# Attention and two feed-forward layers on one core: key and query loads that write all 128 partitions, and a planner that counts 16 transfer engines and instruction fetches

## The chip, the cores and the metric

The kernel runs on one core of a Trainium2 chip, as one program. The metric is the device time of that program in microseconds (us). TensorE (PE in the profile; its weight loads are PEld) does the matrix products; VectorE (DVE), ScalarE (ACT) and GpSimd (POOL) do the rest; SyncE (SP) computes nothing and issues nearly all transfers (DMAs).

## The reference

Attention with two small mixes over the heads, then two feed-forward layers:

```python
scores = scale * np.matmul(q, k.transpose(0, 1, 3, 2))      # 4 x 12 x 448 x 448, head_dim 64
scores = np.einsum('bhij,hg->bgij', scores, w_pre)          # mix over heads
attn = np.exp(scores - scores.max(-1, keepdims=True))
attn = attn / (attn.sum(-1, keepdims=True) + 1e-09)
attn = np.einsum('bhij,hg->bgij', attn, w_post)             # mix over heads
x = np.matmul(attn, v)                                      # to 1792 x 768
h = x @ moe_w_in; g = where(h>=1, h, where(h<=-1, 0, (h+1)**2/4)); x = g @ moe_w_out
h = x @ moe2_w_in; solu = h * softmax(h); x = layernorm(solu) * g_ln @ moe2_w_out
```

## The kernel before

**Two stages.** The attention takes about the first 375 us, the two feed-forward layers the rest. The feed-forward code is not touched by the change, and the text below is on the attention.

**Chunks and tiles.** Four batches of 448 query rows are cut into four chunks each (110, 110, 110 and 118 rows), 16 chunks in all. For a chunk:

- `qk` makes the scores of its 12 heads on PE, two heads at a time: one head's 64 rows of the key and query tiles lie in partitions 0 to 63, the other's in 64 to 127. In the kernel before the two are heads p and p+6. ACT (in chunk 0 also DVE) copies each head's scores out of PSUM (`qk_evac`).
- `remap` moves the copied scores, by one DMA for each head (192 in all), into a tile `sr` in which the 12 heads of one query row lie in neighbouring partitions. It reads 110 or 120 rows and writes 10 partitions.
- `pre` mixes the heads of two query groups (five rows each side) at once on PE. DVE takes the row maximum (`rmax`), ACT the exponential (`expo`), POOL and DVE the normalisation (`guard`, `norm`, `wscale`).
- `post` mixes again on PE: 28 small products in a row, 112 instructions. `evac` copies them out, `av` multiplies with the values, and `store_x` writes the result.

**Words.** All these products are in 32-bit float. One of them is four PE instructions in the program: two weight loads and two products, so the trace has two product records for one product. In the planner's table `WORDS`, a `qk` of two heads or a `pre` is 16 instructions, a `post` 112. PE's instructions come to the core in blocks of 256 (16 KB), by transfers that the profile shows as a queue of kind "instruction". The built program also holds PE instructions that only wait for a semaphore (254 before the change, 272 after it); the planner's table leaves them out.

**The loads.** `load_k` brings the keys of four heads in two DMAs of 64 partitions each; three such loads make a batch. `load_q` brings a chunk's queries, also as two DMAs of 64 partitions. Both are issued on SP, those for chunk 0's queries on ACT. Between the products, `spin` puts 430 ns dummy products on PE in the first two chunks.

**What sets the order.** Every operation is a `Task` with an engine, an estimated duration, a due time (priority) and dependencies; `Order.emit` runs a list scheduler over them and writes each engine's instructions in the order that comes out. The due times and gates are computed from the table `OFFS`, the tile counts stand in `BUFS`. In the kernel before the planner models the transfers as two wires (`wire`, `XFER`), and a block of instructions as landing a fixed time (`FETCH`, 4800 ns) after the one before it.

## Time and profile before

| | before |
|---|---|
| median of 3 runs | 1055.34 us (1051.85 to 1056.74) |
| the profiled execution | 1054.95 us |
| its span from the first to the last instruction | 1053.2 us |
| PE busy | 1021.6 us, 97% of the span |
| DVE, ACT, POOL busy | 750.0, 623.2, 352.6 us |
| mean granted TensorE clock | 0.990 |

The profiled execution is 0.39 us below the median of the runs, and 1.75 us of it lie outside the span. Busy time is the time in which at least one instruction of the engine was running; the idle time of an engine before an instruction is put down to what released that instruction, and "issue" means that nothing that the profile shows was waited for.

### The profile page before, as it was taken

How to read it: one execution, taken by the hardware profiler on the slowest of the kernel's cores; microseconds unless marked ns; L12 is line 12 of the kernel's file. 1: busy time of each engine (PE TensorE's matmuls, PEld its weight loads, DVE VectorE, ACT ScalarE, POOL GpSimd, SP SyncE). 2: the span in 40 equal slices, each digit the busy share in tenths (PEclk: the TensorE clock that was granted, in tenths of full speed). 3: DMA queues.
4: the chain of work that ended last, by engine and by line, in shares of the span. 5: the costliest groups of instructions: out<-in, count | busy, mean ns of one | idle time of the engine just before them, and what ended most of it. 6: DMA issues, size and time to landing. Idle time of an engine off the chain costs nothing.

```text
span 1053.2 us, 27458 instructions
## 1 busy us (share of the span) xinstructions
PE 1021.6 (97%) x11103; PEld 844.0 (80%) x11103; DVE 750.0 (71%) x1258; ACT 623.2 (59%) x1329; POOL 352.6 (33%) x470
## 2 busy tenths in 40 slices
PE   8989998998999999999999999999999999999998
PEld 4555655565665799999999999999999888889998
DVE  3545564655656882588987869898887999888863
ACT  3868885886977675543334434343434577688761
POOL 4111121212211352454555445554521255033210
PEclk9989998999999999999999999999999999999999
DMA  7786676687757450332424232433364646598321
GB/s 187 215 190 191 194 209 194 179 235 200 231 179 231 152 187 21 98 122 81 140 70 140 91 120 90 143 111 102 115 207 163 211 174 242 186 334 315 118 81 60
DMA packets 91358, 171.42 MB, mean 163 GB/s; under 512 B 10220, under 2 KB 66016, under 8 KB 91232
## 3 DMA queue, kind: packets, MB, share of 16 engines
q1 hardware_dynamic: 90816, 169.30, 51.5%
q8 instruction: 88, 1.44, 0.6%
q10 hardware_dynamic: 160, 0.34, 0.2%
q14 instruction: 38, 0.31, 0.1%
q0 software_dynamic: 256, 0.02, 0.0%
HBM read 91.07 MB, written 39.85 MB: 124 GB/s over the span
## 4 chain that ended last, share of the span: by engine, by line
PE 91%; issue 2%; DVE 2%; ACT 2%; DMA 2%; POOL 1%; ACTq 0%; SPq 0%; DVEq 0%; POOLq 0%
PE ps_post L406 7%; PE ps_o L878 7%; PE ps_o L879 7%; PE ps_o L877 7%; PE ps_h L848 7%; PE ps_h L847 7%; PE ps_h L849 7%; PE ps_pre L370 7%; PE ps_av L457 6%; PE ps_qk L336 6%; PE ps_ot L1211 3%; PE ps_ot L1212 3%; PE ps_ot L1213 3%; PE ps_h L1211 3%; PE ps_h L1213 3%; PE ps_h L1212 3%
## 5 line engine op out<-in xcount | busy, mean ns | idle before, releaser
L406 PEld LDWEIGHTS ps_post<-wr,p 64*64 64x64 f32 x5040 | 105.0, 138 | 50.3 <-issue 35.7
L375 DVE TENSOR_REDUCE nm<-ps_pre 128x1 f32<-128x448 f32 x180 | 105.5, 618 | 48.3 <-PE ps_pre L370 45.8
L878 PE MATMUL ps_o<-g,wout 128*128 128x448 f32 x384 | 139.3, 363 | 0.0
L877 PE MATMUL ps_o<-g,wout 128*128 128x448 f32 x384 | 139.1, 362 | 0.0
L879 PE MATMUL ps_o<-g,wout 128*128 128x448 f32 x384 | 138.8, 362 | 0.0
L380 ACT ACTIVATE p<-ps_pre,nm 128x448 f32<-128x448 f32 x180 | 113.1, 637 | 27.1 <-DVE nm L375 26.9
L406 PE MATMUL ps_post<-wr,p 64*64 64x60 f32 x5040 | 106.7, 223 | 13.1 <-issue 12.0
L869 POOL TENSOR_TENSOR g<-t,g 128x448 fp32r<-128x448 f32 x64 | 83.2, 1303 | 100.9 <-ACT g L865 84.1
L887 DVE TENSOR_TENSOR x2acc<-ps_o,x2acc 128x448 f32<-128x448 f32 x168 | 100.2, 616 | 20.9 <-PE ps_o L879 19.6
L766 POOL TENSOR_TENSOR m<-m,v 128x768 f32<-128x768 f32 (+1 forms) x48 | 86.7, 1806 | 80.8 <-DVE v L748 54.3
L370 PE MATMUL ps_pre<-sr,wp 64*64 64x448 f32 (+1 forms) x720 | 100.9, 569 | 5.5 <-ACT at L426 3.2
L336 PE MATMUL ps_qk<-kraw,qb 64*64 64x448 f32 (+2 forms) x768 | 97.2, 543 | 5.7 <-issue 3.8
L354 ACT ACTIVATE s<-ps_qk 119x448 f32<-119x448 f32 (+1 forms) x186 | 91.0, 562 | 17.4 <-PE ps_qk L336 15.6
L387 POOL TENSOR_SCALAR nm<-nm 128x2 f32<-128x2 f32 x90 | 18.5, 206 | 235.3 <-ACT p L380 234.8
L853 ACT ACTIVATE t<-ps_h,st 128x448 f32<-128x448 f32 x64 | 40.4, 631 | 81.4 <-PE ps_h L849 76.7
L738 ACT ACTIVATE v<-v,st 128x768 int32<-128x768 int32 (+1 forms) x48 | 42.2, 880 | 58.0 <-DVE v L734 57.7
L877 PEld LDWEIGHTS ps_o<-g,wout 128*128 128x128 f32 x384 | 72.0, 188 | 5.3 <-DVE x2acc L887 0.2
L878 PEld LDWEIGHTS ps_o<-g,wout 128*128 128x128 f32 x384 | 72.1, 188 | 4.6
L879 PEld LDWEIGHTS ps_o<-g,wout 128*128 128x128 f32 x384 | 72.0, 187 | 4.6
L428 DVE COPY at<-ps_post 128x420 f32<-128x420 f32 x94 | 55.8, 597 | 25.1 <-PE ps_post L406 20.7
L426 ACT ACTIVATE at<-ps_post 128x420 f32<-128x420 f32 x94 | 54.6, 587 | 31.9 <-PE ps_post L406 30.3
L457 PE MATMUL ps_av<-at,vv 128*64 128x240 f32 (+1 forms) x648 | 70.4, 358 | 0.0
(196 smaller groups left out, 2456.9 us busy)
## 6 DMA issues: line engine op xcount, KB each, us to landing
sr<-s SPq DMA_DIRECT2D x144, 192.5 KB
raw<-in_moe_w_out_dram SPq DMA_DIRECT2D x22, 768.0 KB
raw<-in_moe_w_in_dram SPq DMA_DIRECT2D x14, 768.0 KB
sr<-s SPq DMA_DIRECT2D x48, 210.0 KB
xe<-e SPq DMA_DIRECT2D x14, 512.0 KB
el<-xe SPq DMA_DIRECT2D x14, 512.0 KB
raw<-in_moe_w_in_dram SPq DMA_DIRECT2D x12, 512.0 KB
kraw<-in_k_dram SPq DMA_DIRECT2D x24, 224.0 KB
```

The lines of the kernel that those rows point to most:

```text
L336: nc.tensor.matmul(out=qk_t[b, c, p + 6 * e][64 * j:at_], lhsT=qb[rows, i % 2, lo:hi], rhs=kraw_t[b, p][rows], start=True, stop=True,)
L354: nc.scalar.activation(out=s[:n], in_=qk_t.pop((b, c, h))[:n], func=AF.Copy, scale=0.125)
L370: nc.tensor.matmul(out=pre_t[t][o:o + 64], lhsT=wp[k_], rhs=sr[i % 2][k_, g, :], start=True, stop=True)
L375: nc.vector.tensor_reduce(nm_t[t // 2][:, 0, t % 2:t % 2 + 1], pre_t[t], axis=AX.X, op=ALU.max, negate=True)
L380: nc.scalar.activation(out=p, in_=pre_t.pop(t), func=AF.Exp, bias=nm[:, 0, e], accum_out=nm[:, 1, e])
L406: nc.tensor.matmul(out=ps[i][64 * j:64 * j + 64, k, :], lhsT=ps_p[e][64 * i:64 * i + 64, x:x + 64], rhs=wr[64 * i:64 * i + 64, e], start=T ...
L457: nc.tensor.matmul(out=ps[0][64 * j:64 * j + 64, a, :2 * w].rearrange("p (e s c) -> p e s c", e=2, c=SEG), lhsT=v_t[b][:, 1 + m, h * D:(h ...
L766: nc.gpsimd.tensor_tensor(out=m, in0=m, in1=vt.pop(key).bitcast(F32)[:, :n], op=ALU.mult)
L877: nc.tensor.matmul(out=ps, lhsT=wh, rhs=g[:, 0], start=(i == 0), stop=False)
L878: nc.tensor.matmul(out=ps, lhsT=wh, rhs=g[:, 1], start=False, stop=False)
L879: nc.tensor.matmul(out=ps, lhsT=wl, rhs=g[:, 0], start=False, stop=(i == 1))
L887: nc.vector.tensor_tensor(out=dst, in0=op.pop((u, m)), in1=dst, op=ALU.add)
```

## The change

**Keys.** One DMA loads the keys of four heads into all 128 partitions. A unit of `qk` is now heads 2p and 2p+1, since these lie one above the other in the input. **Queries.** The rows of two neighbouring chunks lie side by side in the partitions: `load_q(i, w)` brings one third (four heads) of chunk i into partitions 0 to 63 and the same third of chunk i+1 into 64 to 127. So each chunk's queries are loaded twice, and one half of each copy is used: the even heads from the load of chunk i, the odd heads from that of chunk i-1. Three loads of 128 partitions stand for two of 64. **Spins.** Only one of the two heads of a unit brings a dummy product (10 instead of 20, beside the first five). **The plan.** A class `Wires` keeps 16 transfer engines with their busy times; each transfer costs so much on so many of them, a block of instructions is asked for 320 instructions ahead and goes on one engine of the table `BLOCK_ON`, behind what is queued there. The offsets are other numbers, key tiles go from five to four and `wr` from six to five.

```diff
-OFFS = dict(split=-19.802, pre=0.556, rmax=-10.082, expo=-14.671, guard=36.186, ...
+OFFS = dict(split=-19.802, pre=2.072, rmax=-10.221, expo=-12.343, guard=40.787, ...
-BUFS = dict(kraw=5, q=2, vv=2, s=12, sr=2, p=8, st=8, wr=6, x=3, psa=4, psb=4)
+BUFS = dict(kraw=4, q=6, vv=2, s=12, sr=2, p=8, st=8, wr=5, x=3, psa=4, psb=4)
-BLOCK, FETCH, AHEAD, SWITCH = 256, 4800, 32, 120
-LAND = 1300
-XFER = dict(load_k=lambda *a: (1500, 1200), load_q=lambda *a: (1200, 900), load_v=lambda *a: (1900, 1000),
-            remap=lambda i, b, c, h: (92 * GR[c], 0), e_load=lambda n: (3000, 2300), e_stash=lambda n: (1200, 1000),
+BLOCK, ASKED, PRELUDE, SWITCH = 256, 320, 62, 120
+LAND, DEEP = 1300, 8
+BLOCK_ON = {6: 4, 7: 5, 0: 6, 1: 7, 2: 12, 3: 13, 4: 14, 5: 15}
+XFER = dict(load_k=lambda *a: (1160, 16), load_q=lambda i, w: (650, 16), load_v=lambda b, m: (1000 if m else 1800, 16),
+            remap=lambda i, b, c, h: (72 * GR[c], 10), e_load=lambda n: (2200, 16), e_stash=lambda n: (1000, 16),
...
-                k, late = (sent + AHEAD) // BLOCK + 1, 0
-                while k * BLOCK <= sent + AHEAD + t.words:
...
+                t.dur += wire.fetch(st, t.work, t.words)
+            if e == 'SP':
+                t.dur += wire.room(st)
...
+class Wires:
+    def __init__(self):
+        self.busy, self.words, self.asked, self.out = [0] * 16, PRELUDE, {}, []
+
+    def send(self, at, load, starts):
+        cost, n = load
+        for e in range(n):
+            self.busy[e] = max(self.busy[e], at) + cost
+        end = max(self.busy[:n])
+        self.out += [end + LAND] * starts
+        return end
+
+    def room(self, at):
+        return max(0, self.out[-DEEP] - at) if len(self.out) >= DEEP else 0
+
+    def fetch(self, at, work, words):
+        a, late = self.words, 0
+        self.words += words
+        for x in range((a // 64 + 1) * 64, a + words + 1, 64):
+            t, k = at + late + work * (x - a) // words, (x + ASKED) // BLOCK
+            if (x + ASKED) % BLOCK == 0:
+                e = BLOCK_ON[k % 8]
+                self.busy[e] = max(t + 1200, self.busy[e], self.asked.get(k - 1, 0) - 1500) + 900
+                self.asked[k] = self.busy[e] + 1500
+            elif x % BLOCK == 0:
+                late += max(0, self.asked.get(x // BLOCK, 0) - t)
+        return late
...
     def load_k(b, p):
         t = pl['kraw'].tile([128, 2, S], F32, tag="kraw", name="kraw")
-        heads = k[b].rearrange("p (e d) s -> d (p e) s", e=2)
-        for e in range(2):
-            nc.sync.dma_start(out=t[e * D:(e + 1) * D], in_=heads[:, 6 * e + p:6 * e + p + 2])
+        nc.sync.dma_start(out=t, in_=k[b, p:p + 2].rearrange("j p s -> p j s"))
...
-    def load_q(i, b, c):
-        n = H // 2 * GR[c] * R
-        for e in range(2):
-            (nc.sync if i else nc.scalar).dma_start(out=qb[e * D:(e + 1) * D, i % 2, QPAD:QPAD + n], in_=q[b, c, :, e * n:(e + 1) * n])
+    def load_q(i, w):
+        r0, r1 = (64 if i < 0 else 0), (64 if i == last_q else 128)
+        wide = max(GR[i % 4] if i >= 0 else 0, GR[(i + 1) % 4] if i < last_q else 0) > 11
+        o = 44 * R * w
+        n = QW[w] if wide else 44 * R
...
+        (nc.sync if i > 0 else nc.scalar).dma_start(
+            out=qb[(i + 1) % 2 * 3 + w][r0:r1, at_:at_ + n], in_=q_rows[D * i + r0:D * i + r1, o:o + n])
...
-        for h in (p, p + 6):
+        for h in (2 * p, 2 * p + 1):
...
-                if i < 2 and p >= P['sp0']:
+                if i < 2 and p >= P['sp0'] and not e:
                     add("PE", 430, 1e6, spin, 1, b, c, h, deps=[a2], new=[r_psb], use=[(r_s, -1)])
```

Three places show what the new plan writes. The first is PE's order up to the first `pre`, before the change (a row is line, operation, tiles and shape; `x5` is five of them in a row):

```order
L336 MATMUL ps_qk<-kraw,qb 64x448
L336 MATMUL ps_qk<-kraw,qb 55x448
L345 MATMUL ps_spin<-s 64x256 x2
L336 MATMUL ps_qk<-kraw,qb 64x448
L336 MATMUL ps_qk<-kraw,qb 55x448
...
L345 MATMUL ps_spin<-s 64x256 x5
L370 MATMUL ps_pre<-sr,wp 64x448 x8
```

and after it:

```order
L370 MATMUL ps_qk<-kraw,qb_121 64x448
L370 MATMUL ps_qk<-kraw,qb_121 55x448
L370 MATMUL ps_qk<-kraw,qb_124 64x448
L370 MATMUL ps_qk<-kraw,qb_124 55x448
L379 MATMUL ps_spin<-s 64x256 x2
L404 MATMUL ps_pre<-sr,wp 64x448 x8
```

Before, 48 products of `qk` (both first chunks) and 24 spins (the first five among them) stand ahead of the first `pre`; now it is 40 and 13.

The second place is PE around its 1792nd instruction, where block 7 begins (in the last row of each excerpt); before:

```order
L406 MATMUL ps_post<-wr,p 64x60 x28
L336 MATMUL ps_qk<-kraw,qb 64x448
L336 MATMUL ps_qk<-kraw,qb 60x448
...
L370 MATMUL ps_pre<-sr,wp 64x448 x4
L406 MATMUL ps_post<-wr,p 64x60 x28
L336 MATMUL ps_qk<-kraw,qb 64x448
L336 MATMUL ps_qk<-kraw,qb 60x448
...
L406 MATMUL ps_post<-wr,p 64x60 x28
```

and after:

```order
L440 MATMUL ps_post<-wr,p 64x60 x28
L370 MATMUL ps_qk<-kraw,qb_121 64x448
L370 MATMUL ps_qk<-kraw,qb_121 60x448
...
L404 MATMUL ps_pre<-sr,wp 64x448 x8
L370 MATMUL ps_qk<-kraw,qb_121 64x448
L370 MATMUL ps_qk<-kraw,qb_121 60x448
...
L440 MATMUL ps_post<-wr,p 64x60 x84
```

Before, `post` always came alone (90 times 28 products). Now nine stand as pairs and two as threes, the one shown here among them.

The third place is SP's order where the second batch's keys are loaded, before:

```order
L315 DMA qb<-in_q_dram 64x660 x2
L359 DMA sr<-s 10x12x448 x6
L309 DMA kraw<-in_k_dram 64x2x448 x2
L359 DMA sr<-s 10x12x448 x4
L309 DMA kraw<-in_k_dram 64x2x448 x2
L359 DMA sr<-s 10x12x448 x2
L309 DMA kraw<-in_k_dram 64x2x448 x2
L315 DMA qb<-in_q_dram 64x660 x2
```

and after:

```order
L334 DMA kraw<-in_k_dram 128x2x448
L393 DMA sr<-s 10x11x448
L348 DMA qb_123<-in_q_dram 128x440
L356 DMA vv<-in_v_dram 128x768
L393 DMA sr<-s 10x11x448
L334 DMA kraw<-in_k_dram 128x2x448 x2
L348 DMA qb_124<-in_q_dram 128x440
L393 DMA sr<-s 10x12x448 x12
```

The key loads moved ahead of the last chunk's twelve remaps, and thirds of the queries stand between them.

## Rows read from the trace of the kernel before

**Rows 1.** The page: busy time by engine, instruction queue, chain by engine.
```profile
PE 1021.6 (97%) x11103; PEld 844.0 (80%) x11103; DVE 750.0 (71%) x1258; ACT 623.2 (59%) x1329; POOL 352.6 (33%) x470
...
q8 instruction: 88, 1.44, 0.6%
...
PE 91%; issue 2%; DVE 2%; ACT 2%; DMA 2%; POOL 1%; ACTq 0%; SPq 0%; DVEq 0%; POOLq 0%
```

**Rows 2.** Windows: stretch, length, busy time (instructions) by engine, clock, DMA share, GB/s.
```profile
0.00:375.00 375.00, 348.27 (x7658) 220.06 (x7658) 214.58 (x470) 278.72 (x755) 84.68 (x213) 0.97 0.71 198
375.00:1053.20 678.20, 673.28 (x3451) 623.95 (x3449) 535.42 (x788) 344.51 (x574) 267.96 (x258) 1.00 0.42 143
```

**Rows 3.** Waits of PE: line, released by: us in total, times, longest.
```profile
PE ps_post L406 <- issue: 12.0, 8, 4.5
PE ps_qk L336 <- issue: 3.8, 2, 3.2
```

**Rows 4.** Timeline of PE: start, length, instruction, records [idle before, released by].
```profile
51.69 0.93 PE L406 MATMUL ps_post<-wr,p 64*64 64x60 f32 x30
53.09 0.62 PE L406 MATMUL ps_post<-wr,p 64*64 64x60 f32 x26 [0.46 <-issue]
...
61.75 1.43 PE L406 MATMUL ps_post<-wr,p 64*64 64x60 f32 x42 [3.42 <-issue]
...
162.16 1.43 PE L406 MATMUL ps_post<-wr,p 64*64 64x60 f32 x41 [4.47 <-issue]
...
249.59 0.58 PE L336 MATMUL ps_qk<-kraw,qb 64*55 64x448 f32 x1 [3.18 <-issue]
```

**Rows 5.** DMA queues and issues from 51.6 to 59 us: no row of kind instruction.
```profile
q1 hardware_dynamic: 776, 1.48, 82.4%
...
sr<-s SPq DMA_DIRECT2D x4, 210.0 KB
...
qb<-in_q_dram SPq DMA_DIRECT2D x2, 165.0 KB
```

**Rows 6.** DMA queues from 58.9 to 60.3 us.
```profile
q8 instruction: 1, 0.02, 4.9%
```

**Rows 7.** Windows behind the three longest waits of rows 4.
```profile
61.80:71.50 9.70, 9.44 (x192) 6.28 (x194) 4.79 (x11) 4.33 (x11) 1.16 (x4) 0.54 0.77 184
...
162.20:167.00 4.80, 4.80 (x61) 3.13 (x65) 0.74 (x2) 1.76 (x5) 0.19 (x1) 0.56 0.57 175
...
249.70:258.00 8.30, 7.69 (x126) 4.48 (x126) 3.71 (x10) 4.52 (x15) 0.58 (x2) 1.00 0.83 227
```

**Rows 8.** Windows: 64-partition loads at the start, 128-partition loads from 375 us.
```profile
2.00:6.00 4.00, 4.00 (x11) 1.73 (x11) 0.00 (x0) 1.24 (x1) 4.00 (x8) 1.00 0.99 213
...
375.00:390.00 15.00, 15.00 (x108) 13.96 (x107) 11.61 (x16) 9.56 (x17) 7.91 (x8) 1.00 0.76 242
```

**Rows 9.** Timeline of SP at the start.
```profile
0.73 4.08 SPq L309 DMA_DIRECT2D kraw<-in_k_dram  x6
...
10.65 1.24 SPq L315 DMA_DIRECT2D qb<-in_q_dram  x2
12.00 7.71 SPq L359 DMA_DIRECT2D sr<-s  x9
```

**Rows 10.** Timeline of PE at the first `pre`.
```profile
23.98 2.10 PE L345 MATMUL ps_spin<-s 64*64 64x256 f32 x9
25.78 0.60 PE L370 MATMUL ps_pre<-sr,wp 60*64 60x448 f32 x3
```

**Rows 11.** The chain that ended last: start, us, engine, records; one transfer in it.
```profile
38.66 1.04 PE ps_post L406 x56
...
50.89 0.98 PE ps_pre L370 x8
...
86.46 1.50 PE ps_qk L336 x16
...
231.62 3.84 DMA sr<-s
```

More of the change, by code (lines that the diff above doesn't have):

```diff
@@ L105, in dma @@
         d.issue = t
-        d.load = XFER.get(fn.__name__, lambda *a: (xfer, xfer))(*a)
+        d.load = XFER.get(fn.__name__, lambda *a: (xfer, 16))(*a)
         return d
@@ L146, in emit @@
         avail, free = {}, {}
-        sent, landed, was, wire, slow = 0, {}, False, [0, 0], 0
+        was, wire, slow = False, Wires(), 0
         for t in self.tasks:
@@ L205, in give @@
                 if o.eng == 'DMA':
-                    wire[:] = [max(w, o.ready) + x if x else w for w, x in zip(wire, o.load)]
                     o.start = o.ready
-                    o.dur = max(w for w, x in zip(wire, o.load) if x) - o.ready
+                    o.dur = wire.send(o.ready, o.load, STARTS.get(t.fn[0].__name__, 1) if t.eng == 'SP' else 0) - o.ready
                     done.append(o)
@@ L264, in attention @@
     wk = const.tile([128, H, HR], F32, name="wk")
-    qb = const.tile([128, 2, QPAD + H // 2 * 120], F32, name="qb")
+    qb = [pl['q'].tile([128, QPAD + QW[w]], F32, name=f"qb{j}{w}") for j in range(2) for w in range(3)]
     at = const.tile([128, KB, H, 3 * SEG], F32, name="at")
@@ L271, in zero_w @@
         nc.gpsimd.memset(wp, 0.0)
-        nc.gpsimd.memset(qb[:, :, :QPAD], 0.0)
+        for t in qb:
+            nc.gpsimd.memset(t[:, :QPAD], 0.0)
         nc.gpsimd.memset(wb, 0.0)
@@ L327, in qk @@
     def qk(i, b, c, p):
[L328 to L329 removed]
+        n, w = GR[c] * HR, p // 2
+        for h in (2 * p, 2 * p + 1):
             qk_t[b, c, h] = pl['psa'].tile([128, S], F32, tag="a", name="ps_qk")
[L331 removed]
         for e in range(2):
[L333 removed]
+            rows, src = slice(D * e, D * e + D), qb[(i + 1 - e) % 2 * 3 + w]
+            o = QPAD + (40 * w if GR[c] > 11 else 0) + (2 * (p % 2) + e) * 2 * n
             for j in range(2):
@@ L336, in qk @@
                 nc.tensor.matmul(
-                    out=qk_t[b, c, p + 6 * e][64 * j:at_], lhsT=qb[rows, i % 2, lo:hi], rhs=kraw_t[b, p][rows],
+                    out=qk_t[b, c, 2 * p + e][64 * j:at_], lhsT=src[rows, lo:hi], rhs=kraw_t[b, p][rows],
                     start=True, stop=True,
@@ L624, in attention @@
         t0 = t
-        n = GR[c] * R
         if i:
-            pr = t0 + P['sq'] - 3 if i > 1 else -99
-            q0 = od.dma("SP", 1250, 2000, pr, load_q, i, b, c, new=[r_q], deps=held if i == 1 else ())
-            gates.append((q0, pr if i > 2 else P['q2'] if i == 2 else -1))
+            for w in range(3):
+                pr = t0 + P['sq'] + P['qs'] * w if i > 1 else P['q1'] + P['qs'] * w
+                q_d[i, w] = od.dma("SP", 600, 2000, pr, load_q, i, w, new=[r_q])
+                if i > 1:
+                    gates.append((q_d[i, w], pr if i > 2 else P['q2']))
         rms = []
@@ L633, in attention @@
             if c == 0 and p % 2 == 0:
-                kt[b, p // 2] = od.dma("SP", 1300, 1240, pr + P['sk'] - 2 if b else -100, load_k, b, p, new=[r_kraw])
+                kt[b, p // 2] = od.dma("SP", 650, 1240, pr + P['sk'] - 2 if b else -100, load_k, b, p, new=[r_kraw])
                 if b:
                     gates.append((kt[b, p // 2], pr + P['sk'] - 2))
-                if i == 0 and p == 0:
-                    q0 = od.dma("Activation", 1250, 2000, -100, load_q, i, b, c, new=[r_q])
-            a1 = add("PE", 754, pr, qk, i, b, c, p, deps=[q0, kt[b, p // 2]], new=[r_psa, r_psa],
-                     use=[(r_q, i), (r_kraw, b * H // 4 + p // 2)])
+            w = p // 2
+            if i == 0 and p == 0:
+                for x in range(3):
+                    q_d[-1, x] = od.dma("Activation", 600, 2000, -100 + 2 * x, load_q, -1, x, new=[r_q])
+                for x in range(3):
+                    q_d[0, x] = od.dma("Activation", 600, 2000, -99 + 2 * x, load_q, 0, x, new=[r_q])
+            a1 = add("PE", 754, pr, qk, i, b, c, p, deps=[q_d[i, w], q_d[i - 1, w], kt[b, w]], new=[r_psa, r_psa],
+                     use=[(r_q, 3 * i + 3 + w), (r_q, 3 * i + w), (r_kraw, b * H // 4 + w)])
             for e in range(2):
-                h = p + 6 * e
+                h = 2 * p + e
                 en, dur = ("DVE", 550) if i == 0 and e else ("Activation", 470)
                 a2 = add(en, dur, pr + P['qks'] * e, qk_evac, b, c, h, en, deps=[a1], new=[r_s], use=[(r_psa, -1 if e else -2)])
-                if i < 2 and p >= P['sp0']:
+                if i < 2 and p >= P['sp0'] and not e:
                     add("PE", 430, 1e6, spin, 1, b, c, h, deps=[a2], new=[r_psb], use=[(r_s, -1)])
@@ L648, in attention @@
                                   new=[] if rms else [r_sr], join=[r_sr] if rms else []))
-                if i == 0 and len(rms) == P['hold']:
-                    held = [rms[-1].issue]
         if i == 0:
```

32 lines of the change are left out of this document (15 added, 17 removed).

## The prediction

> **What bounds the kernel now.** I read the page first: PE is busy 97% of the span, and the chain that ended last runs through PE for 91%; the next entry, "issue", has 2% [rows 1]. Then the two stages by windows. The feed-forward layers, from 375 us, leave PE 4.9 us of idle time in 678, and nothing of them is changed: for them I take no change. The attention leaves 375.0 - 348.3 = 26.7 us of PE idle, at a mean clock of 0.97 [rows 2]. ACT (278.7) and DVE (214.6) have room there. So the change can win only in three places: in those 26.7 us, in the missing clock, and in PE work that is dropped.
>
> The waits of PE say what the idle time is: most of it is "issue", 12.0 us before `post` and 3.8 us before `qk` [rows 3], and most of that is three gaps, of 3.42, 4.47 and 3.18 us, together 11.07 [rows 4]. "Issue" names no cause, so I asked the transfer queues. The 88 packets of the instruction queue stand for 22206 PE instructions (11103 products and 11103 weight loads), 252 each [rows 1]: these are PE's program blocks. Counting PE's instructions in the program's order, with those that only wait and 62 ahead of the program (the planner's `PRELUDE`), block 6 begins at the 31st record of a `post`; PE's `post` at 51.69 breaks off after 30 records and goes on at 53.09 after 0.46 us of "issue" [rows 4]. So the count holds. The planner takes it that a block is asked for 320 instructions ahead; for block 7, which begins at 1792, that is at the end of the `pre` ahead of this same `post`, near 51.6 us. From 51.6 to 59 us no instruction packet moved, while 82% of the transfer engines' time went to others, remaps and a query load among them [rows 5]. One moved between 58.9 and 60.3, for 4.9% of 16 engines in 1.4 us, 1.1 us [rows 6], and PE went on at 61.75. So PE ran dry at 58.3 because its next block was queued for about 7 us. By the same count the other two gaps stand where blocks 24 and 39 begin.
>
> Two of the gaps cost more than themselves: behind the first PE had a mean clock of 0.54 for 9.44 busy us, behind the second 0.56 for 4.80 us; behind the third it stayed at 1.00 [rows 7]. [...] The loss is 9.44 x 0.46 + 4.80 x 0.44 = 4.3 + 2.1 = 6.4 us.
>
> [...]
>
> **The change, part by part.**
>
> *Key and query transfers.* A batch's keys are six transfers of 64 x 2 x 448 numbers of 4 bytes, 1.38 MB, before and after. While only 64-partition loads ran, the engines were 0.99 busy for 213 GB/s, 215 at full share; 128-partition loads later gave 242 at 0.76, 318 at full share [rows 8]. The price of a 128-partition key load from this input isn't in the trace; its bounds are these two. At 215 the keys cost the engines 6.4 us a batch as now, at 318 4.3. I take 318, since that row has 128 partitions and the other has 64. A chunk's queries grow from 330 KB (two of 165 [rows 5]) to three loads of 128 partitions by 440 columns of 4 bytes, 676 KB (799 beside wide chunks): 1.5 us now, 2.1 to 2.5 at 318, 3.1 to 3.7 at 215. For a chunk, keys -0.5 and queries +0.6 to +1.0 come to about +0.3 us of transfer time in 375/16 = 23.4 us, or +2 us at the bad end. The engines are 0.71 busy [rows 2]: this hides, and I cost it at nothing; where it doesn't hide is in a fetch's queue, below. A query third may be loaded only once the same third of the chunk before is done on PE, so it has four of six `qk` units, about 15 us, against the 3.84 us that one remap took to land in a crowded stretch [rows 11]. Key tiles fall from five to four, so the first load of the next batch still has a free one and the others wait for the last chunk's units; that leaves them a chunk's rest, some 8 us or more. Both at nothing. On SP a batch's six key issues (4.08 us [rows 9]) become three, and a chunk's two query issues (1.24 us [rows 9]) three: -2.0 and +4 x 0.6 us in 94. Nothing.
>
> *Start.* The first `pre` runs at 25.78 us behind nine spin records of 2.10 us without a gap [rows 10]. What it needs is chunk 0's twelve remaps; SP issued the last nine up to 19.71 [rows 9]. With a landing of 1.6 to 3.84 us (the lower end is what is left from the packet to PE's restart in [rows 4, 6], the upper the crowded remap of [rows 11]) it could start between 21.3 and 23.6. After the change 11 spins and two `qk` units fewer stand ahead of it, and SP's order of these twelve remaps has as much between them as before (two query issues). A spin is two records, and records follow each other 2.10/9 = 0.23 us apart: ten spins fewer in all are 20 x 0.23 = 4.6 us of PE work. PE can't keep more than the remaps leave: 2.2 to 4.5 us. I take **-3**, nearer the lower end, since thinner cover leaves some idle.
>
> *The plan.* If it does its work, the three gaps (11.1) and the two slow stretches (6.4) go: **-17.5** at most. What bounds it is how much PE work lies between a block's call and its need. I counted that from the order with [rows 11]: a `post` 1.04 us, a `pre` 0.98, a `qk` unit 0.75. For block 7 before: the end of a `pre` (0.1), `post` 1.04, `qk` 0.75, `pre` 0.98, `post` 1.04, two `qk` 1.5, 27 instructions of `post` (0.25), 5.7 us. After: 41 instructions of `post` (0.4), `qk` 0.75, two `pre` 1.96, two `qk` 1.5, then a `post` and 83 instructions of the next in the triple (1.8), 6.4 us. For blocks 24 and 39 the same count gives 6.4 to 8.7 and 6.9 to 7.6. But the bunched `post`s thin others out. In the attention two blocks before had less than 5.4 us, the least 5.0; the sixth, with 5.2, has the 0.46 us of [rows 4]. After, eleven have 3.9 to 5.0. By `BLOCK_ON` eight of them come on engines 12 to 15, which the plan keeps free of remaps, and three (30, 33, 41) on 4 to 7, where blocks 7, 24 and 39 were late. One thing speaks against the plan's aim: it counts no waiting instructions, so that its blocks are 33 instructions off at block 7 and 196 of 256 at the end of the attention. In its second half it guards the wrong places.
>
> *What comes back.* The trace can't show the new waits. Below: nothing, if the queues at those eleven blocks are short. Above: each waits as block 7 did, 3.4 us. I take 8 x 0.3 = 2.4 us for those on quiet engines, just below the 0.46 of the thin block that there is; 3 x 2 = 6 for those on the remaps' engines, midway between 0.46 and 3.4; and half of one long gap with its slow stretch (17.5/3 = 5.8), 2.9. Together **+11**.
>
> Sum: 1054.95 - 17.5 - 3 + 11 = 1045.5, in the profiled execution's own time; that lies 0.39 us below the median of the runs. I say **1045**.
>
> **Rivals.**
>
> *The gaps stay.* The queue of 7 us is made by remaps, which the change leaves as they are, and the real transfers and block starts lie otherwise than the plan's. Then only the start is won: 1054.95 - 3 = 1052. For it: 0.7 us more room at block 7 is far less than 7, and the drift of the plan's count. Against: two query loads and four long remaps moved in that stretch [rows 5], and what stands close together there the new plan can space out.
>
> *All is won.* Nothing comes back: 1034.5. For it: all three blocks win room, two of them little. Against: eleven thin blocks.
>
> *Slower.* The bunched `post`s run dry. Place: the eleven thin blocks, whose engines every key, value and query load now uses. Price: at 2 us each and two slow stretches of 4.3, 22 + 8.6 = 31, so 1054.95 - 20.5 + 31 = 1065. It decides from a mean wait of 20.5/11 = 1.9 us at the thin blocks. For it: a block has waited 7 us in a queue. [...]
>
> **How the numbers follow.** Forecast (1038 to 1050, the likeliest's own range) 0.46; all won (below 1038) 0.14; gaps stay (1050 to 1058) 0.24; slower (above 1058) 0.16. The range from 1034 to 1062 leaves out about 0.06 below and 0.13 above. Half a percent, about what a measurement of this kernel can tell from no change, is 5.3 us: faster is below 1050.1, the first two cases, 0.60; slower is above 1060.6, 0.14; the rest, 0.26, is same.
>
> **What would show it.** Right: no PE gap over 3 us by "issue" in the attention, clock 0.98 or more there, first `pre` at 21 to 24 us, PE idle in the attention near 18 us, the feed-forward stretch as long as before. Transfers: in the first microseconds more GB/s at the same share. Wrong if long "issue" gaps stand at other blocks, above all behind the paired and triple `post`s, or if PE waits for query or key loads by name.

## The result, and the profile after

| | before | after |
|---|---|---|
| median of the runs beside each other | 1055.49 us | 1067.14 us |
| ratio, with its 95% interval | 1 | 1.0101 (1.0056 to 1.0147) |
| the profiled execution, its span | 1054.95, 1053.2 us | 1066.41, 1064.6 us |
| mean granted TensorE clock | 0.990 | 0.990 |

The change made the kernel about 1% slower, and 1067 us is outside the range that was forecast (1034 to 1062), on the other side of before. The ratios leave out runs more than 1.5% above the fastest of the same kernel, here the 1078.97 us of the four runs after. The two stages of the profile after, in the columns of [rows 2] (stretch, length, busy time of PE, PEld, DVE, ACT, POOL, clock, DMA share, GB/s):

```profile
0.00:375.00 375.00, 333.35 (x7455) 206.21 (x7459) 206.60 (x457) 273.04 (x740) 81.48 (x214) 0.97 0.70 207
...
390.00:1064.60 674.60, 669.69 (x3401) 620.32 (x3399) 536.38 (x782) 343.06 (x570) 263.68 (x256) 1.00 0.42 143
```

The feed-forward stage leaves PE 4.9 us idle, as in [rows 2]; it only begins later, so the loss is in the attention. The clock there is 0.97 as before in these two executions; over the runs of all experiments it is not the same (see the last table). The waits of PE up to 395 us (line, released by: us in total, times, longest) answer to [rows 3]:

```profile
PE ps_post L440 <- issue: 15.1, 10, 5.3
PE ps_av L491 <- issue: 7.9, 3, 4.8
PE ps_qk L370 <- DMA qb<-in_q_dram: 4.7, 3, 2.2
PE ps_pre L404 <- DMA qb<-in_q_dram: 3.9, 1, 3.9
PE ps_pre L404 <- issue: 2.0, 1, 2.0
```

"Issue" did not go away: with a last 0.3 us before `qk` it is 25.3 us against 16.4 before. And PE now waits by name for transfers, 8.6 us against 0.7. Together that is 16.8 us more. Other waits are 1.5 us less (6.9 against 8.4), and ten dummy products fewer take some 4.6 us of PE work away; the span grew by 11.4. The timeline of PE at the first `pre` and at the three longest waits (start, length, instruction, records, idle before and its releaser) answers to [rows 4, 10]:

```profile
27.73 1.77 PE L404 MATMUL ps_pre<-sr,wp 64*64 64x448 f32 x8 [3.94 <-DMA qb<-in_q_dram]
...
71.16 1.13 PE L440 MATMUL ps_post<-wr,p 64*64 64x60 f32 x33 [5.31 <-issue]
...
208.99 0.81 PE L440 MATMUL ps_post<-wr,p 64*64 64x60 f32 x39 [3.36 <-issue]
...
251.07 1.38 PE L491 MATMUL ps_av<-at,vv 128*64 128x240 f32 x8 [4.83 <-issue]
```

By the count that the prediction used these are blocks 7, 31 and 38. Block 7, late before, is later now: it began at 61.75 us in [rows 4] and begins at 71.16 now. The DMA view from 59 to 68.5 us says what lay ahead of that block (queue: packets, MB, share of 16 engines; then the transfers issued, KB each), beside [rows 5]:

```profile
q1 hardware_dynamic: 1231, 2.18, 98.0%
...
kraw<-in_k_dram SPq DMA_DIRECT2D x2, 448.0 KB
qb<-in_q_dram SPq DMA_DIRECT2D x2, 220.0 KB
vv<-in_v_dram SPq DMA_DIRECT2D x1, 384.0 KB
sr<-s SPq DMA_DIRECT2D x1, 210.0 KB
sr<-s SPq DMA_DIRECT2D x1, 192.5 KB
```

No row of kind instruction in 9.5 us again, and now the engines are 0.98 busy: 1.7 MB of keys, queries and values and two remaps were issued there, where before two query loads of 165 KB and four remaps stood. PE waited 5.31 us in front of the block.

One part did what was forecast of it. At the start, with mostly 128-partition loads moving, three query loads of 64 partitions among them (window in the columns above):

```profile
1.00:7.00 6.00, 4.75 (x14) 2.28 (x18) 0.00 (x0) 1.28 (x1) 6.00 (x16) 1.00 0.94 278
```

That is 278/0.94 = 296 GB/s at full share, against 213/0.99 = 215 in [rows 8].

The start, too, was not won. PE from 20 to 40 us (columns as above), in the kernel before:

```profile
20.00:40.00 20.00, 19.56 (x365) 11.87 (x363) 9.25 (x19) 16.55 (x43) 2.50 (x9) 1.00 0.83 216
```

and after:

```profile
20.00:40.00 20.00, 14.94 (x250) 7.16 (x254) 7.55 (x15) 9.91 (x26) 2.31 (x8) 0.83 0.64 183
```

With fewer products and dummy products ahead of the first `pre`, PE was busy 2.93 of the 7.7 us before it, and then the clock was 0.50 from 27.7 to 31.1 us.

The waits of SP show what the prediction left out. The rows of SP in front of its query loads, for PE's scores, in the kernel before:

```profile
SPq L315 <- PE ps_qk L336: 3.9, 6, 1.9
```

and after:

```profile
SPq L348 <- PE ps_qk L370: 22.3, 16, 5.3
```

For these 22 us SP stood in front of a query load whose tile was not free, with the remaps and loads that follow it in SP's order behind it. That this delayed PE is not shown by the row: in this execution no `pre` waited for a remap by name. And SP stands longer elsewhere in both kernels, 41.8 us before and 36.4 after in front of stores of results.

### The profile page after: what moved, and what is told of

Same layout as the page of the kernel before. It is cut to its first block, busy times and chain, and to the rows that moved or that the text cites. A ratio compares the mean times of both kernels' runs of the same rounds, so it can differ in the third digit from the quotient of the medians.

```text
span 1064.6 us, 27427 instructions
## 1 busy us (share of the span) xinstructions
PE 1017.7 (96%) x11083; PEld 839.3 (79%) x11083; DVE 756.1 (71%) x1258; ACT 625.7 (59%) x1329; POOL 350.9 (33%) x475
## 4 chain that ended last, share of the span: by engine, by line
PE 87%; DMA 4%; issue 4%; DVE 2%; ACT 2%; POOL 0%; SPq 0%; ACTq 0%; DVEq 0%; POOLq 0%
PE ps_post L440 7%; PE ps_o L916 7%; PE ps_o L915 7%; PE ps_o L914 7%; PE ps_h L886 7%; PE ps_h L885 7%; PE ps_h L884 7%; PE ps_pre L404 7%; PE ps_qk L370 6%; PE ps_av L491 5%; PE ps_ot L1250 3%; PE ps_ot L1248 3%; PE ps_ot L1249 3%; PE ps_h L1248 3%; PE ps_h L1249 3%
## 5 line engine op out<-in xcount | busy, mean ns | idle before, releaser
L440 PEld LDWEIGHTS ps_post<-wr,p 64*64 64x64 f32 x5040 | 96.0, 137 | 52.6 <-issue 36.2
L409 DVE TENSOR_REDUCE nm<-ps_pre 128x1 f32<-128x448 f32 x180 | 102.5, 616 | 46.6 <-PE ps_pre L404 44.6
L414 ACT ACTIVATE p<-ps_pre,nm 128x448 f32<-128x448 f32 x180 | 112.7, 640 | 34.5 <-DVE nm L409 32.6
L440 PE MATMUL ps_post<-wr,p 64*64 64x60 f32 x5040 | 102.6, 223 | 19.6 <-issue 15.1
L404 PE MATMUL ps_pre<-sr,wp 64*64 64x448 f32 (+1 forms) x720 | 97.3, 561 | 7.2 <-DMA qb<-in_q_dram 3.9
L886 PE MATMUL ps_h<-sr,win 128*128 128x448 f32 x192 | 69.7, 363 | 0.0
```

Source lines behind the costliest of these rows:

```text
L404: nc.tensor.matmul(out=pre_t[t][o:o + 64], lhsT=wp[k_], rhs=sr[i % 2][k_, g, :], start=True, stop=True)
L409: nc.vector.tensor_reduce(nm_t[t // 2][:, 0, t % 2:t % 2 + 1], pre_t[t], axis=AX.X, op=ALU.max, negate=True)
L414: nc.scalar.activation(out=p, in_=pre_t.pop(t), func=AF.Exp, bias=nm[:, 0, e], accum_out=nm[:, 1, e])
L440: nc.tensor.matmul(out=ps[i][64 * j:64 * j + 64, k, :], lhsT=ps_p[e][64 * i:64 * i + 64, x:x + 64], rhs=wr[64 * i:64 * i + 64, e], start=T ...
L886: nc.tensor.matmul(out=ps, lhsT=wl, rhs=xh, start=False, stop=(kk == 5))
```

## The experiments

All ratios are to the kernel before, run beside each, with 95% intervals. A table of the waits of the kernels with whole remaps on SP stands at the end of this section.

**The two halves of the change.** The new loads with the planner of before and its offsets, but for three of the query loads (`sq` 3 groups earlier, `q1` and `qs` as after) and new prices for key and query loads; the tile counts are those of after:

```diff
-OFFS = dict(split=-19.802, pre=2.072, ... expo=-12.343, ... sq=-28.177, ... qk0=-9.874, ...
+OFFS = dict(split=-19.802, pre=0.556, ... expo=-14.671, ... sq=-30.965, ... qk0=-14.645, ...
-class Wires:
...
+                    landed[k + 1] = max(at, landed.get(k, 0)) + FETCH
```

> The new loads (keys and query thirds in 128 partitions, doubled query bytes, six query tiles, 10 spins) with the planner, the offsets and the transfer costs of before; tile counts as after the change. If the doubled query bytes make the loss, it stays: 1062 us or more, with the first pre again after 27 us. If the new plan makes it, the time goes back to 1056 us or less, and the first pre comes before 26 us.

Measured: 1.0096 (1.0060 to 1.0132), first `pre` at 26.26 us. The new planner and offsets with the loads and tile counts of before:

```diff
+OFFS = dict(split=-19.802, pre=2.072, ... qk0=-9.874, ...
+XFER = dict(load_k=lambda *a: (2130, 16), load_q=lambda *a: (1550, 16), ...
+class Wires:
```

> The loads of before (two DMAs of 64 partitions, each query once, 20 spins) with the new planner and its offsets; a key pair costs 2130 ns and a chunk's queries 1550 ns on 16 engines. If the doubled query bytes make the loss, this is at 1056 us or less with the first pre before 26 us. If the new plan makes it (bunched posts, fewer instructions counted than there are), this stays at 1062 us or more, with issue gaps of 3 us and over.

Measured: 1.0140 (1.0099 to 1.0180). Each half alone costs as much as both, so the two losses don't add up, and the loss can't be put down to one half. Even with the loads of before, SP waits 17.1 us in front of query loads under the new plan, so that wait doesn't need the new tiles.

**The bytes of the queries.** Only the heads that are used, as two 64-partition DMAs for each third (a confound: nine issues on ACT at the start instead of six, and the tiles are zeroed):

```diff
+            dst = t[D * e:D * e + D, at_:at_ + 4 * n2].rearrange("d (h n) -> d h n", h=4)
+            eng.dma_start(out=dst[:, e::2], in_=src[:, e::2])
```

> The changed kernel, but of each query third only the heads that are used are loaded: the even ones into partitions 0 to 63, the odd ones into 64 to 127, two DMAs with runs of 440 or 480 bytes, half the bytes. If the bytes make the loss, most of it goes: 1057 us or less and the first pre 2 us earlier than in the changed kernel (27.7). If it is the reuse of the query tiles (a third can be loaded only when the chunk before is done with it), or the plan, it stays at 1062 us or more.

Measured: 1.0104 (1.0072 to 1.0135). Half the bytes bring nothing back, but the confound shows: the first `pre` runs at 29.16 us, 1.4 later than after. SP's waits in front of query loads fell here to 8.9 us, and PE still waited 16.0 us for transfers.

**Remaps with half of their columns,** in the kernel after and in the kernel before. From the fifth chunk on these kernels leave out half of the columns of the copied scores, so they only show what the remaps cost:

```diff
-        n = GR[c] * HR
+        n, m = GR[c] * HR, S if i < 4 else S // 2
...
-            out=sr[i % 2][pad + h:pad + H * R:H, :GR[c], :], in_=s_t.pop((b, c, h))[64 - n:64 + n]
+            out=sr[i % 2][pad + h:pad + H * R:H, :GR[c], :m], in_=s_t.pop((b, c, h))[64 - n:64 + n, :m]
```

> The changed kernel, but from the fifth chunk on each remap moves only the first 224 of the 448 columns; the other half of the mixed scores is that of older chunks. If the long issue gaps come from remaps queued ahead of the instruction blocks, no issue gap over 1 us is left after 80 us, and the time falls by 10 us or more, below 1057. If the bunched posts are too dense for the blocks by themselves, gaps of 1 us and more stay there and the time falls by less than 4 us.

> The kernel before with the second half of the columns left out of every remap from the fifth chunk on, as in the run with half remaps of the kernel after (about 1042 us). Theory (remaps queued ahead of instruction blocks cost both kernels; what the change lost lies in the first 70 us and in which blocks are hit): before loses its three long gaps behind issue too and some slow clock, so 1036 to 1042 us, and the 12 us between the kernels shrink to 3 to 6, those of the start. Rival (the new order itself keeps TensorE waiting, whatever the remaps cost): the distance of 12 us stays, so about 1030 us. Rival (before suffered little from the remaps): 1048 us or more, and after gains its 25 us only because its plan had brought the queue about.

Measured: after 0.9867 (0.9831 to 0.9902), 1042.43 us; before 0.9839 (0.9791 to 0.9886), 1039.82 us. The waits of PE in the kernel after with half remaps:

```profile
PE ps_qk L370 <- DMA qb<-in_q_dram: 5.6, 2, 3.8
PE ps_post L440 <- issue: 4.1, 6, 1.2
PE ps_pre L404 <- DMA qb<-in_q_dram: 2.1, 1, 2.1
PE ps_av L491 <- issue: 1.7, 1, 1.7
```

"Issue" fell from 25.3 to 6.5 us, in before from 16.4 to 5.4 (behind 80 us two gaps over 1 us are left in after, 1.7 and 1.1): in both kernels these waits are mostly made by what remaps leave in the queues. Not all of the fall is theirs. The shorter remaps begin at about 85 us; from there on "issue" fell from 16.0 to 4.9 us and from 11.9 to 1.3. Up to there the work is the same as at full size, and yet the kernel after had 9.3 us of "issue" in one profile and 1.6 in the other, with 5.31 and 1.20 us in front of block 7: a single execution's "issue" scatters by that much. And the distance between the two kernels, 1.0% at full size, is 0.28% here, give or take 0.6. So the loss seems to need remaps of full size, at the edge of what the intervals tell; the waits for queries stay.

**The blocks' bounds.** Tiny matmuls at the start, unknown to the planner, leave every order as it is and move the bounds of all later blocks. In the kernel after 16 or 32 of them, four words each, came on top of the five dummy products:

```diff
+        for _ in range(SHIFT if h is None else 0):
+            nc.tensor.matmul(out=ps[:64, :16], lhsT=wp, rhs=wp[:, :16], start=True, stop=True)
```

> The kernel after with 16 more tiny matmuls (16 columns each) in the first idle time of TensorE, unknown to the planner: every engine's order stays as it is, but all later TensorE instructions lie 64 words further on in the 256-word blocks. Theory (which work stands in a block on engines 4 to 7 when remaps are queued there decides the gaps): the gaps over 2 us come at other places than 65.85, 205.63 and 246.24, and the time moves by up to 8 us either way with the same order. Rival (the gaps belong to the order of the work, not to the blocks' bounds): gaps at the same places within a microsecond of the same work, time within 3 us of after.

> As the shift by 64 words, with 32 tiny matmuls, 128 words, half a block. Theory: gaps over 2 us at other places again, the time up to 8 us off that of after and not the same as with 64 words. Rival: gaps and time as after, within 3 us.

Measured: 1.0150 (1.0094 to 1.0206) and 1.0167 (1.0108 to 1.0227). The tiny products took longer than meant and moved the first `qk` from 6.7 to 8.8 and 12.2 us, and the first `pre` from 27.7 to 28.3 and 32.3, so 0.6 and 4.6 us of it are the start's. The gaps went elsewhere, as the theory had it: with 64 words "issue" is 11.5 us, but one `pre` waits 8.18 us for a remap (timeline of PE, then of SP):

```profile
263.77 1.01 PE L407 MATMUL ps_pre<-sr,wp 64*64 64x448 f32 x2 [8.18 <-DMA sr<-s]
```

```profile
249.89 3.30 SPq L396 DMA_DIRECT2D sr<-s  x3
253.77 0.39 SPq L527 DMA_DIRECT2D xs<-x  x1
255.46 0.33 SPq L540 DMA_DIRECT2D eraw<-in_moe_w_out_dram  x1
257.12 0.79 SPq L396 DMA_DIRECT2D sr<-s  x1
```

Ahead of the remap in SP's order stand a store of results and a weight load of 768 KB, issued 1.7 us before it; that these held it up is not shown. The same in the kernel before, with 13 or 21 tiny products in place of the five, so that the start keeps its length (first `qk` at 5.4 and 5.5 us):

```diff
-        for _ in range(n):
+        for _ in range(TINY if h is None else 0):
+            nc.tensor.matmul(out=ps[:64, :16], lhsT=wp, rhs=wp[:, :16], start=True, stop=True)
+        for _ in range(0 if h is None else n):
```

> The kernel before, its five warming matmuls at the start replaced by 13 tiny ones of 16 columns: nothing else changes, but all later TensorE instructions lie 32 words further on in the 256-word blocks. Theory (the times and offsets of before fit its own block bounds; any other fit costs about what the change costs): gaps at other places, 1058 to 1068 us, ratio 1.003 to 1.012. Rival (the order of before is better whatever the bounds): gaps may move, but the time stays within 0.4% of before.

> As the shift of before by 32 words, with 21 tiny matmuls, 64 words further on, a start of about the same length as the five of before. Theory (before fits its own bounds): 1058 to 1070 us, three or four gaps over 2 us at other places than 58.33, 157.69 and 246.41. Rival (the order decides): within 0.4% of before.

Measured: 0.9975 (0.9944 to 1.0006) and 0.9980 (0.9943 to 1.0017). My theory fell: the gaps moved, "issue" was 14.3 and 21.1 us, the longest wait 5.0 and 3.8, and the time stayed. Before is not a lucky fit to its bounds.

**The planner's costs, and a nudge.** After, planned with a dearer remap and the waiting instructions counted; and before with seven offsets moved by 0.3:

```diff
-WORDS = dict(qk=16, pre=16, post=112, av=32, spin=4)
+WORDS = dict(qk=16, pre=17, post=113, av=32, spin=4)
-            remap=lambda i, b, c, h: (72 * GR[c], 10), ...
+            remap=lambda i, b, c, h: (96 * GR[c], 10), ...
```

> The kernel after, planned with 96 instead of 72 ns for a remap's packet and with the waiting instructions counted (post 113 words, pre 17): nothing but the order changes. Theory (the planner sees too short a queue on engines 4 to 7): with nearer costs the long gaps shrink; idle time of TensorE behind issue falls from some 25 us to about 17, time 1055 to 1062 us. Rival (offsets were tuned for the other costs, and no such model hits the blocks): 1063 to 1075 us, with as many gaps at other places.

```diff
-... pre=0.556, rmax=-10.082, expo=-14.671, norm=-7.738, post=4.738, sq=-27.965, qk0=-14.645 ...
+... pre=0.856, rmax=-9.782, expo=-14.371, norm=-7.438, post=5.038, sq=-27.665, qk0=-14.345 ...
```

> The kernel before with seven of its offsets moved by 0.3 of a group (0.6 us of plan), loads and planner as they were: part of the order changes (some 560 of 4,000 rows on TensorE), nothing in its manner. Theory that before is a picked order (any new order of this work costs about 1%, and the change's 1% is no more than that): ratio 1.006 to 1.015. Theory that the change's own parts cost it (query loads that stop SyncE, scores placed late, the loads between a chunk's remaps): ratio 0.997 to 1.004, SyncE's waits in front of query loads for TensorE's scores still 5 us or less.

Measured: 1.0060 (1.0011 to 1.0110) and 0.9997 (0.9968 to 1.0026). The first ratio flatters: the medians of all runs, 1067.48 and 1058.13 us, give 1.0088, and 1067.48 is in the rival's range. Nearer costs took "issue" from 25.3 to 14.5 us, as the theory had it, but waits for transfers rose to 13.4. The nudge speaks against before being a picked order: one other order of its manner costs nothing. Orders as far from it as that of the change were not tried with its loads and planner. Its SP waits in front of query loads are 1.8 us.

**Every third remap from GpSimd.** The planner of after books a remap on the ten lowest of its 16 engines. In the kernel before, from 18 to 19.8 us, with only remaps issued on SP, the transfer engines were 0.66 busy, as many as 10.5 of 16; which ones no row shows. On the kernel before:

```diff
-        nc.sync.dma_start(
+        (nc.gpsimd if i > 1 and h % 3 == 2 else nc.sync).dma_start(
```

> The kernel before, with every third remap from the third chunk on issued by GpSimd instead of SyncE, so that its packets may go by another queue and other engines than the low ten. Theory (remaps queued on the ten low engines ahead of instruction blocks cost some 15 us): if these remaps spread over other engines, idle time behind issue falls by a third or more, 1045 to 1053 us. Rival (the remaps of GpSimd land later, some 7 us after their issue as its small loads do at the start, and GpSimd issues them ahead of the scales that post waits for): pre waits for remaps, 1065 to 1090 us.

Measured: 1.0451 (1.0411 to 1.0491), 1103.83 us, beyond the rival's range, and not by its wait: PE waited 1.6 us for transfers, and 40.3 for ACT and other engines. GpSimd's own waits:

```profile
POOL sr L359 <- ACT s L354: 44.5, 25, 6.9
```

It stood 44.5 us in front of remaps whose scores ACT had not yet copied, with the scales that `post` needs behind them. "Issue" of PE fell only from 16.4 to 14.2 us. Of the 192 remaps 56 were issued on GpSimd and 136 on SP; whether those of GpSimd went by other engines stays open.

**The waits for transfers.** From here I had a new theory, told in the expectations. Scores of a chunk placed as early as in before; the first query halves in the still free second `sr` tile; and both:

```diff
-   qk0=-9.874, qks=0.465, dmalat=2100, sk=-16.738, ...
+   qk0=-14.645, qks=0.449, dmalat=2100, sk=-11.967, ...
```

```diff
+    def q_tile(i, w):
+        return sr[1][:, 2 * w:2 * w + 2].rearrange("p g s -> p (g s)") if i < 0 else qb[(i + 1) % 2 * 3 + w]
```

> The kernel after with the score products of a chunk placed as far ahead of their pre as in before (qk0 -14.645 instead of -9.874, qks 0.449; key loads kept where they were). The new theory (waits behind issue are about equal in both kernels, wherever the blocks' bounds lie; what the change adds are waits for transfers, the remaps' because the scores are computed some 4.8 groups later): waits of pre for remaps fall to 2 us or less, as in before; waits for queries at the start stay at 5 to 9 us; ratio to before 1.002 to 1.007. Rival (the offsets belong together, and one of them alone only makes another bad fit): 1.010 or more.

> The kernel after with the first chunk's upper query halves in the second remap buffer, which is still free, so that the second chunk's three query loads wait for no tile and are issued together behind the third remap. New theory: TensorE's waits for queries fall from some 8 us to 4 us or less, those for remaps stay; first pre 25 to 27 us; ratio 1.004 to 1.008. Rival (the start is bound by the bytes of keys, queries and remaps together): the wait moves to the remaps, first pre 27 us or later, ratio as after, 1.008 to 1.013.

> Both edits together in the kernel after. New theory: both waits for transfers are mostly gone, ratio 0.996 to 1.003, about as before; what is left are the waits behind issue, some 15 us. Rival: 1.008 or more, as after.

Measured: 1.0174 (1.0139 to 1.0209), 1.0086 (1.0054 to 1.0118) and 1.0171 (1.0121 to 1.0220). With early scores no `pre` waits for a remap by name, as forecast (16.3, 2.4 and 9.4 us in the two shifts of after and with dearer remaps; but none in after itself), while waits for queries rose from 8.6 to 22.2 us, which was not forecast. The two kernels with early scores fell on the rival's side, and the first queries alone at the edge between the two. One place of the run with early scores alone, SP's timeline and then PE's:

```profile
216.06 0.38 SPq L524 DMA_DIRECT2D xs<-x  x1
216.95 0.84 SPq L348 DMA_DIRECT2D qb<-in_q_dram  x1
```

```profile
221.82 1.76 PE L370 MATMUL ps_qk<-kraw,qb 64*64 64x448 f32 x8 [3.79 <-DMA qb<-in_q_dram]
```

The load is issued 4.9 us ahead of its use. By the code, a tile that holds rows of two chunks comes free a chunk later than before, so with two sets the scores can be early only if queries are late. The first queries alone took PE's waits for transfers from 8.6 to 5.2 us, and the time hardly moved.

**A third query set.** It needs 6 KB a partition, taken from the tiles of copied scores; that alone is the control:

```diff
-BUFS = dict(kraw=4, q=6, vv=2, s=12, ...
+BUFS = dict(kraw=4, q=6, vv=2, s=8, ...
```

```diff
-BUFS = dict(kraw=4, q=6, vv=2, s=12, ...
+BUFS = dict(kraw=4, q=9, vv=2, s=8, ...
-            out=qb[(i + 1) % 2 * 3 + w][r0:r1, ...
+            out=qb[(i + 1) % 3 * 3 + w][r0:r1, ...
```

> The kernel after with 8 instead of 12 tiles for the copied scores, which makes room for the next run; the control for it. Both theories: within 0.5% of after, ratio to before 1.006 to 1.015; SyncE still waits some 20 us in front of query loads for the scores of TensorE (22.3 us, 16 times, in after; 3.9 us, 6 times, in before).

> As the control with 8 score tiles, but with three sets of query tiles instead of two, so that a query load no longer waits for the scores of the chunk before last but one. New theory (each set of after holds rows of two chunks and comes free a chunk later; SyncE then stands still in front of query loads with remaps behind them): SyncE's wait in front of query loads falls from some 20 us to under 6 us, TensorE's waits for transfers to 4 us or less, ratio 1.000 to 1.006. Rival (SyncE's waits there cost nothing; bytes and blocks' bounds set the time): they fall, and the ratio stays at 1.008 to 1.015.

> As the run with three query sets, and with the scores as far ahead of pre as in before (qk0 -14.645, qks 0.449). New theory: no waits for remaps and few for queries, ratio 0.994 to 1.003, against 1.017 for early scores with two sets. Rival (early scores fit these loads badly in any case, or 8 score tiles are too few for them): 1.010 or more.

Measured: control 1.0171 (1.0132 to 1.0210), which should have been as after and wasn't; three sets 1.0132 (1.0081 to 1.0184); three sets and early scores 1.0133 (1.0087 to 1.0180), against 1.0174 with two. SP's waits in front of query loads went from 16.8 to 2.4 and 0.3 us, as forecast, and 0.4% came back, inside the intervals; 1% was expected. With three sets alone PE's waits for transfers did not fall to 4 us: they were 12.0, against 9.2 in the control. So PE waited for transfers there without SP's stops, and by the time both kernels came out on the rival's side. The waits of PE in the last one:

```profile
PE ps_post L440 <- ACT p L414: 8.1, 21, 1.9
PE ps_post L440 <- issue: 7.6, 5, 3.4
PE ps_pre L404 <- DVE at L462: 6.5, 8, 1.3
PE ps_qk L370 <- DMA qb<-in_q_dram: 3.4, 3, 1.9
```

Waits for transfers and "issue" together are 17.0 us, before's level; but PE now waits 21.4 us for ACT, DVE and others. That the offsets of the new plan, made for late scores, bring these about is an argument and was not tested.

**The kernels with whole remaps on SP in one table** (us of PE's waits up to 395 us in the profiled execution, summed by kind; SP's wait in front of query loads for PE's scores; the mean granted clock of the runs in the ratio, for before by experiment):

```
kernel                               ratio    issue  transfers  others   SP    clock
before                               1         16.4     0.7       8.4    3.9   0.993 to 0.995
before nudged                        0.9997    16.5     2.1      12.8    1.8   0.995
before, 32 and 64 words on           0.9975    14.3     6.5       9.7    1.8   0.995
                                     0.9980    21.1     2.3       9.9    1.9   0.995
after                                1.0101    25.3     8.6       6.9   22.3   0.991
after, 64 and 128 words on           1.0150    11.5    24.6       5.0   31.7   0.985
                                     1.0167    16.9    15.7       4.7   30.4   0.985
after, dearer remaps                 1.0060    14.5    13.4       4.6   33.7   0.989
new loads, plan of before            1.0096    12.9     8.9      12.0   20.8   0.989
new plan, loads of before            1.0140    17.6    12.6       9.6   17.1   0.988
after, half of the query bytes       1.0104    14.3    16.0       6.5    8.9   0.984
after, first queries apart           1.0086    24.8     5.2       6.0   23.8   0.989
after, early scores                  1.0174     9.6    22.2      11.5    9.6   0.985
after, both                          1.0171    13.3    16.0       7.8   19.7   0.987
after, eight score tiles             1.0171    17.0     9.2      11.3   16.8   0.989
after, three sets                    1.0132    12.3    12.0      13.0    2.4   0.989
after, three sets, early scores      1.0133    12.9     4.1      21.4    0.3   0.994
```

"Issue" has no sign: 14 to 21 us in the four of before, 10 to 25 in the others. Waits for transfers are mostly higher with the change, 4.1 to 24.6 against 0.7 to 6.5, but they don't go with the ratio: 8.9 and 12.0 us stand beside 1.0096 and 1.0132, 4.1 beside 1.0133. What parts the two groups better is the sum of all three, 25.5 to 33.3 us in the four of before and 32.5 to 43.3 in the others. A single execution scatters (that of the new loads with the plan of before was the shortest of its runs, 1059.46 against a median of 1067.83), so the rows are to be read as groups.

The last column, over all runs, holds a part of the loss that no column of waits has: 0.993 to 0.995 in the kernels of before, 0.984 to 0.991 with the change, but for the last row. As an estimate, 0.006 of 1060 us is 6 us, over half of the 1%, if PE was at work in all of that time. In the kernel after the clock fell behind long waits of PE (0.83 from 71.2 to 80 us, behind the 5.31 us of block 7), so it may be the price of the waits rather than a cause of its own; no run here tells the two apart.

## Why the prediction was wrong

**The plan, -17.5: this step failed.** The reading of the gaps held (blocks queued behind data; half remaps take most of them away in both kernels), but not that moving work by a plan would remove them. The gaps came back at other blocks: "issue" was 25.3 us instead of the 5 that would be left without the three, and about 10 us or more in every kernel at full work. 0.7 us more room at block 7 met 9.5 us without an instruction packet instead of 7, in a stretch in which the new order issued 1.7 MB of loads. The 6.4 us of slow stretches were not won either: the clock was 0.60 from 27.7 to 34.5 us and 0.83 from 71.2 to 80. With what comes back, the prediction had -6.5 us here; the profile has +8.9 of "issue" and no gain in clock. That is about 15 of the 21 us between the forecast 1045 and the profiled 1066.41, with the scatter of single executions in it. The rival "the gaps stay" had this step right, with its own argument, but not the loss.

**What comes back, +11: wrong place.** I charged it to eleven thin blocks, most on engines 12 to 15 of `BLOCK_ON`. The three longest waits are at blocks 7, 31 and 38, none of them among the eleven, by `BLOCK_ON` on engines 5, 5 and 4, on which the planner has remaps too; which engine a block really goes by, no run here shows. The rival "slower" gave 1065 us by those thin blocks; its number was near, its mechanism not what the trace shows, so that was luck.

**Loads and SP at nothing: failed too, 7.9 us.** The faster transfer was right, and so was the rule that a query third may be loaded only once the chunk before is done with it. I weighed the 15 us of that rule against the landing of one remap, 3.84 us, and did not ask who is queued behind the waiting load on SP. In the profile after SP stood 22.3 us there instead of 3.9, and PE waited 8.6 us for transfers instead of 0.7; in the kernels of the changed family it is up to 24.6. That the one makes the other is not shown: with three query sets SP's wait was gone and PE still waited 12.0 us, at a ratio of 1.0132.

**Start, -3: failed.** First `pre` at 27.73 us instead of 21.3 to 23.6. SP issued chunk 0's last remap by 20.08, close to the 19.71 of [rows 9]; what I had wrong is what follows, at most 3.84 us by my rows. Between 20.1 and 27.7 lie 7.6. The profile names a query load there, which `pre` doesn't read; by the code the last remap is what it needs, so I take the 7.6 us for its landing. A kernel with the same start had the first `pre` at 24.9 (half remaps), so the term is about zero and uncertain by 1.5 us or so. And behind the thinner cover, from which I expected some idle time, the clock was lower as well, 0.83 from 20 to 40 us, where before had 1.00.

**Feed-forward at no change: right.**

So shown: most of the gaps come from what is queued (with half remaps "issue" from 85 us on fell from 16.0 to 4.9 us in after, from 11.9 to 1.3 in before), and the plan did not remove them; either half of the change brings the loss without the other; and before is not a lucky fit to its blocks' bounds (shifted, no change) or to one order (nudged, no change). The bytes of the queries are unlikely (halved, no gain, though with a later start). With half remaps the distance nearly closes. Shown as an effect of the edits, too: with two sets, early scores bring PE's waits for queries from 8.6 to 22.2 us. What makes the 1% is open. My last theory, waits for transfers behind SP's stops, failed where it was tried: with the stops gone 0.4% came back against its control, within the intervals, and with the waits for transfers at 4.1 us as well it was no more, while waits for ACT and DVE had taken their place. Not tried apart are the clock (lower in all but one of the change's kernels), the ten dropped dummy products, and the smaller tile counts; the new plan with the loads of before has neither of the last two and loses as well, so they are not needed for it. What stays open, too, is whether offsets fitted to three query sets would bring the kernel to before's time or below; no version of the change at full work did.

## What to carry to other kernels

When a load gets a new rule for when its buffer is free, ask also what is queued behind that load on the issuing engine, and read the waits of that queue by releaser. But a long wait found there is a suspect, not a cause, until a run takes it away: here it fell from 16.8 to 2.4 us, and the time by 0.4%, inside the intervals. Gaps that come from a shared queue need not go when work is moved around them: here halving the remaps took 11 us of "issue" away from 85 us on in both kernels, where the new plan took none. Compare such sums over several executions, since the same work left 9.3 us in one and 1.6 in another, and set the granted clock of all runs beside them. And before a slower order is called bad luck, shift and nudge the faster one: two shifts and one nudge of before cost nothing, which speaks against luck.

## What the runs showed of the hardware that was not expected

At the start the transfers ran at 296 GB/s at full share with mostly 128-partition loads and at 215 with 64-partition ones, and the kernel was no faster for it. For 9.5 us with the engines 0.98 busy no packet of PE's instructions moved, and PE stood 5.31 us. And the first 25 us of two programs with the same work up to there differed by 3 us (first `pre` at 24.9 and 27.7 us).
